# Row scales of the first output weights: sums of sizes on ScalarE in place of maxima on VectorE

## The chip, the cores and the metric

The kernel runs on one core of one Trainium2 chip. The metric is device time in microseconds (us) of one execution, median of three runs. Engines: TensorE (PE; its weight loads are PEld), VectorE (DVE), ScalarE (ACT), GpSimd (POOL), and SyncE (SP), whose queue issues the DMAs. Each engine works through its own queue of instructions.

## The reference

Attention over 4 batches and 12 heads, then two MLPs on the 1792 tokens. All inputs arrive as float64.

```python
q_n, k_n = rmsnorm(q, g_q), rmsnorm(k, g_k)              # 4 x 12 x 448 x 64
attn = softmax(q_n @ k_n.T / sqrt(64)); attn_out = attn @ v
x = attn_out.transpose(0, 2, 1, 3).reshape(1792, 768)
h = x @ w_in;  x = (h * sigmoid(1.702 * h)) @ w_out      # first MLP, 768 -> 2048 -> 768
h = x @ w_in2; x = (max(h, 0) + alpha * min(h, 0)) @ w_out2
```

## The kernel before

**Weights.** A float64 matrix is read as pairs of 32-bit words (DMA into a ring of raw tiles). `from_words` makes float32 of them: `fold`, a Prelu on ScalarE (L147), then a shift (L163) and a shift-and-or (L164) on VectorE. Each row of a weight matrix then gets a power of two as its scale: a maximum of the row's absolute values (L244, VectorE), `row_scales` (L104, L105 and L171, tiny VectorE operations), and `split_rows` writes the scaled row as two float16 halves, the high one on ScalarE (L178), the low one on VectorE (L179). When all rows are there, `weight_scales` takes the largest scale over partitions (a small TensorE matmul `pm`, L119) and makes a `ratio` for every row. The matmuls run three float16 products per pair (high-high, high-low, low-high).

**The first output weights** `w1o` are 2048 x 768: 16 row blocks of 128 x 768 (`nj` = 16), two loads each, in groups of two (`G1O`). Their generator `w1o_steps` is advanced while the second half of batch 0's attention runs, six pairs of heads with two units each. The float32 numbers of block j lie in the place of block j + 2 of `w1o`, so block j's own place is free by then.

**What else runs in that stretch.** For every unit: scores (PE `sp`, L490), their maxima (DVE `nm`, L504), the exponent (ACT `pr`, L523, with a sum read out), transposes (PE `tp`, L580), their copies (ACT `ptf`, L585), the values (PE `xp`, L616). Beside them `first_in` starts the first MLP on batch 0's first 256 tokens: it needs `x`, which `first_x` splits with the scale `first_sc` (DVE L646; ACT L139, DVE L140), then 18 matmuls `hp` (L720), a tanh (ACT `t`, L731) and a product (DVE `g`, L732) for each of 16 column blocks. After that the same for the other 192 tokens.

**The restart.** Batch 1's attention begins when q and k of its first pair have been squared and summed (ACT L395, DVE L397), their inverse roots computed on POOL (L398 to L408), scaled (DVE `qk`, L418), split (`hl`, ACT L451, DVE L452) and transposed by a DMA (`t<-hl`). Its first scores are `sp`, L499. At the same time VectorE and ScalarE split batch 0's `g` with the ratios of `w1o` (L809, L139, L140), for the second matmul `yp` (L790).

**Order.** The code is written as interleaved generators; the framework's scheduler then sets each engine's order when the program is built, from priorities and its own estimates of durations. A changed operation can therefore move others around it.

Of the kernel before, what the change touches and what calls it, by code (L numbers as in the profile page):

```python
# [13 lines left out]
AF = mybir.ActivationFunctionType  # L14
ALU = mybir.AluOpType
AX = mybir.AxisListType.X
# [28 lines left out]
R1O = 4  # L45
G1I = 1
G1O = 2
# [9 lines left out]
def attention_moe_kernel(  # L57
# [17 lines left out]
    nc = tc.nc  # L75
# [100 lines left out]
    def split_rows(w, num, inv, j):  # L176

        nc.scalar.activation(out=w[:, j, 0], in_=num, func=AF.Copy, scale=inv[:, j:j + 1])  # L178
        nc.vector.scalar_tensor_tensor(  # L179
            out=w[:, j, 1], in0=num, scalar=inv[:, j:j + 1], in1=w[:, j, 0], op0=ALU.mult, op1=ALU.subtract  # L180
        )
# [17 lines left out]
        done[nm] = mx, ratio  # L199
        yield  # L200

    def weights(src, nm, w, num_tile, raw_tile, parts, ahead, c, done, group, hold=0):


        rows, cols = src.shape
        words = src.bitcast(I32).rearrange("r (n t) -> r n t", t=2)
        nj = rows // 128
        m = cols // parts
        rm = const.tile([128, nj], F32, name=f"rm_{nm}")
        inv = const.tile([128, nj], F32, name=f"inv_{nm}")  # L210
        raws = []
        nums = []

        def load():
            t = len(raws)
            if t < nj * parts:
                j, i = divmod(t, parts)
                raw = raw_tile(t)
                src_words = words[j * 128:(j + 1) * 128, i * m:(i + 1) * m]
                if len(raw.shape) == 4:  # L220
                    src_words = src_words.rearrange("r (a n) t -> r a n t", a=raw.shape[1])
                loads.setdefault(nm, []).append(nc.sync.dma_start(out=raw, in_=src_words))
                raws.append(raw)

        def split_all():
            while nums:
                split_rows(w(), nums[0][1], inv, nums[0][0])
                nums.pop(0)
                yield

        for _ in range(ahead):
            load()
        yield
        for j in range(nj):
            if hold and j == hold:
                yield "held"
                yield from split_all()
            num = num_tile(j)
            for i in range(parts):
                from_words(num[:, i * m:(i + 1) * m], raws[j * parts + i])  # L240
                load()
                yield
            nums.append((j, num))
            nc.vector.tensor_reduce(out=rm[:, j:j + 1], in_=num, op=ALU.max, axis=AX, apply_absolute_value=True)  # L244
            if (j + 1) % group == 0:
                row_scales(rm, inv, slice(j + 1 - group, j + 1))
                yield
                if j >= hold:
                    yield from split_all()
        if hold:  # L250
            yield "rows"
        yield from weight_scales(nm, rm, nj, c, done, W2I_WAIT if hold else 0)

    def later_rows(w, d, other):

        nj = w.shape[1]
        return lambda j: w[:, j + d].rearrange("p e n -> p (e n)").bitcast(F32) if j + d < nj else other(j)

    scales = {}
# [884 lines left out]
    if True:  # L1144
# [10 lines left out]
        parts = stage[:, 0:R1I * 1024].bitcast(I32).rearrange("p (i n t) -> p i n t", i=R1I, t=2)  # L1155
# [7 lines left out]
        def num1o(j):  # L1163
# [7 lines left out]
        )  # L1171
        w1o_steps = weights(
            moe_w_out, "w1o", lambda: w1o, later_rows(w1o, 2, num1o), lambda t: raw1o[:, 4 * (t % R1O):4 * (t % R1O) + 4], 2,
            R1O, 2.0 ** -25, scales, G1O
        )
        next(w1i_steps)
        normalize(0)
# [43 lines left out]
        done = 4 * NP  # L1221
# [46 lines left out]
```

## Time and profile before

| | |
|---|---|
| time, median of 3 runs | 1184.49 us (1184.01 to 1185.91) |
| the profiled execution: its own time, its span | 1184.74 us, 1183.0 us |
| PE busy | 1073.3 us, 91% |
| DVE busy | 819.6 us, 69% |
| ACT busy | 673.3 us, 57% |
| POOL busy | 79.7 us, 7% |

The shares are averages over stages that are limited by different things. The `w1o` rows are made between about 105 and 206 us of the span, and that stretch has to be read by itself: in the view of stretches, where each engine's busy time stands for given bounds; in the timelines, where an idle time and what ended it stand in brackets; and in the groups by line, for the duration of one instruction.

### The profile page before, as it was taken

The page shows a single profiled execution, that of the slowest core. Times are in us where ns is not written, and L with a number is a line of the kernel's source. Part 1 is how long each engine was busy: PE and PEld are TensorE (multiplying, and loading weights), DVE is VectorE, ACT ScalarE, POOL GpSimd, SP SyncE. Part 2 cuts the span into 40 slices and gives each one's busy share as a digit, 9 for nine tenths or more (in the row PEclk, how much of TensorE's full clock was granted, in tenths as well). Part 3 has the DMA queues.
Part 4 walks back from the last instruction along what each step waited for, and adds up shares of the span by engine and source line. Part 5 has one row for each costly group of instructions (what it writes and reads, how often), then busy time and mean ns, then how long its engine had stood idle before and what let it go on. Part 6 is the DMA issues. An engine that isn't in the chain of part 4 may idle for free.

```text
span 1183.0 us, 18327 instructions
## 1 busy us (share of the span) xinstructions
PE 1073.3 (91%) x6755; PEld 586.6 (50%) x6755; DVE 819.6 (69%) x1445; ACT 673.3 (57%) x1348; POOL 79.7 (7%) x200
## 2 busy tenths in 40 slices
PE   3468799688789989999998999999999999999998
PEld 1234467554344444545454545544444467666665
DVE  6989999986767886467741868489996322978351
ACT  4667776787767875578742545256555423655220
POOL 2300001442011101100000000000000000000000
PEclk9579799899999999999998999999999999999999
DMA  7944542569888685666553821275624423353111
GB/s 232 266 144 137 150 135 77 113 138 182 160 158 157 136 157 121 122 122 115 93 128 65 307 92 52 99 255 178 224 78 144 142 72 123 99 173 101 34 30 31
DMA packets 256458, 158.06 MB, mean 134 GB/s; under 512 B 177648, under 2 KB 239728, under 8 KB 256368
## 3 DMA queue, kind: packets, MB, share of 16 engines
q1 hardware_dynamic: 256368, 156.89, 50.9%
q8 instruction: 53, 0.87, 0.3%
q14 instruction: 37, 0.30, 0.1%
HBM read 92.22 MB, written 25.69 MB: 100 GB/s over the span
## 4 chain that ended last, share of the span: by engine, by line
PE 32%; DVE 20%; DMA 10%; ACT 10%; issue 5%; SPq 3%; POOL 2%; ACTq 0%; POOLq 0%; DVEq 0%
PE op L1052 16%; PE h L892 7%; PE yp L790 5%; ACT pr L523 3%; DVE ph L592 3%; PE hp L767 3%; DVE nm L504 2%; ACT ph L565 2%; SPq L598 2%; DMA yr<-y_dram 2%; DMA qk<-in_q_dram 1%; DMA pt<-ph 1%; DMA t<-hl 1%; DVE g L140 1%; DMA vst<-in_v_dram 1%
## 5 line engine op out<-in xcount | busy, mean ns | idle before, releaser
L790 PE MATMUL yp<-g,w1o 128*128 128x448 f16 x1152 | 228.2, 355 | 1.9 <-DVE g L140 1.6
L892 PE MATMUL h<-x,w2i 128*128 128x512 f16 (+1 forms) x1152 | 218.9, 352 | 2.7 <-DVE pos L898 1.7
L767 PE MATMUL hp<-x,w1i 128*128 128x448 f16 x864 | 172.1, 356 | 3.7 <-DVE t L776 1.8
L892 PEld LDWEIGHTS <-w2i 128*128 128x128 f16 x1152 | 112.6, 98 | 108.1 <-issue 3.5
L790 PEld LDWEIGHTS <-w1o 128*128 128x128 f16 x1152 | 109.8, 98 | 111.8 <-issue 13.2
L767 PEld LDWEIGHTS <-w1i 128*128 128x128 f16 x864 | 82.8, 99 | 88.2 <-issue 15.7
L592 DVE SCALAR_TENSOR_TENSOR ph<-pr,sm,ph 128x448 f16<-128x448 f32 x126 | 86.9, 717 | 20.2 <-ACT ph L565 19.3
L504 DVE TENSOR_REDUCE nm<-sp 128x2 f32<-128x896 f32 x96 | 92.4, 963 | 0.4 <-PE sp L499 0.4
L523 ACT ACTIVATE pr<-sp,nm,c_s 128x448 f32<-128x448 f32 x126 | 90.0, 717 | 2.8 <-DVE ph L592 1.0
L897 ACT ACTIVATE pos<-h,sign 128x512 f32<-128x512 f32 (+1 forms) x64 | 40.2, 629 | 86.0 <-PE h L892 80.2
L565 ACT ACTIVATE ph<-pr,sm 128x448 f16<-128x448 f32 x126 | 77.8, 659 | 18.3 <-DVE sm L562 15.3
L1052 PEld LDWEIGHTS <-even 128*128 128x128 f16 x672 | 65.7, 98 | 43.4
L898 DVE SCALAR_TENSOR_TENSOR pos<-h,slope,pos 128x512 f32<-128x512 f32 (+1 forms) x64 | 43.4, 680 | 57.9 <-ACT pos L897 57.9
L720 PE MATMUL hp<-x,w1i 128*128 128x256 f16 (+1 forms) x576 | 63.9, 273 | 10.0 <-DVE t L732 4.8
L499 PE MATMUL sp<-t 64*128 64x448 f16 (+1 forms) x432 | 56.2, 365 | 17.0 <-ACT pr L523 17.0
L1052 PEld LDWEIGHTS <-odd 128*128 128x128 f16 x504 | 49.3, 98 | 32.6
L616 PE MATMUL xp<-pt,vs 128*64 128x256 f16 (+1 forms) x792 | 50.2, 271 | 16.6 <-DMA pt<-ph 8.4
L1052 PE MATMUL op<-w2lo,even 128*128 128x384 f16 x384 | 63.4, 326 | 0.0
L720 PEld LDWEIGHTS <-w1i 128*128 128x128 f16 x576 | 54.6, 103 | 17.5 <-issue 12.9
L140 DVE SCALAR_TENSOR_TENSOR g<-t,ratio_w1o,g 128x448 f16<-128x448 f32 x64 | 47.0, 736 | 15.0 <-ACT g L139 14.9
L506 ACT ACTIVATE nm<-nm,c_s 128x2 f32<-128x2 f32 x72 | 20.9, 290 | 62.4 <-DVE nm L504 62.2
L616 PEld LDWEIGHTS <-vs 128*64 128x64 f16 x792 | 39.3, 114 | 33.7 <-issue 18.7
(228 smaller groups left out, 1553.8 us busy)
## 6 DMA issues: line engine op xcount, KB each, us to landing
g<-in_moe_w_in_dram SPq DMA_DIRECT2D x24, 512.0 KB, 5.7
g<-in_moe_w_out_dram SPq DMA_DIRECT2D x32, 384.0 KB, 3.7
w2raw<-in_moe_w_in_dram SPq DMA_DIRECT2D x24, 512.0 KB, 5.6
w2raw<-in_moe_w_out_dram SPq DMA_DIRECT2D x16, 768.0 KB, 6.3
g_dram<-pos SPq DMA_DIRECT2D x48, 256.0 KB, 2.0
gp<-g_dram SPq DMA_DIRECT2D x8, 1024.0 KB, 6.7
odd<-g_dram SPq DMA_DIRECT2D x6, 1024.0 KB, 5.4
y_dram<-y SPq DMA_DIRECT2D x24, 224.0 KB, 2.5
```

What stands on the lines that cost most here:

```text
L140: nc.vector.scalar_tensor_tensor(out=dst[1], in0=src, scalar=scale, in1=dst[0], op0=ALU.mult, op1=ALU.subtract)
L499: nc.tensor.matmul(out=sp[:, j, 0:S] if n == 2 else sp[ds, 0, 0:S], lhsT=qt[ds] if n == 2 else qt[ds, 64:128], rhs=kt[ds, 0:S], start=(i = ...
L504: nc.vector.tensor_reduce(out=nm[:, 0:n], in_=sp[:, 0:n, 0:S], op=ALU.max, axis=AX, negate=True)
L523: nc.scalar.activation(out=pr[i], in_=sp[:, i, 0:S], func=AF.Exp, bias=nm[:, i:i + 1], scale=c_s if u >= 4 * NP else 1.0, accum_out=sm[:, ...
L565: nc.scalar.activation(out=ph[:, i, 0:S], in_=pr[i], func=AF.Copy, scale=sm[:, i:i + 1])
L592: nc.vector.scalar_tensor_tensor(out=ph[:, i, S:2 * S], in0=pr[i], scalar=sm[:, i:i + 1], in1=ph[:, i, 0:S], op0=ALU.mult, op1=ALU.subtract)
L616: nc.tensor.matmul(out=xp[64 * j:64 * j + 64, t:t + n], lhsT=vs[ks, j, c], rhs=pt[ks, kc, o:o + n], start=(i == 0), stop=(i == len(steps) ...
L720: nc.tensor.matmul(out=ps, lhsT=w1i[:, kk, e, m * 128:(m + 1) * 128], rhs=xs[0, kk][:, f, cols], start=(i == 0), stop=(i == 3 * KD - 1))
L767: nc.tensor.matmul(out=ps, lhsT=w1i[:, kk, e, m * 128:(m + 1) * 128], rhs=x[:, f], start=(n == 0), stop=(n == 3 * KD - 1))
L790: nc.tensor.matmul(out=ps, lhsT=w1o[:, m, e, j * 128:(j + 1) * 128], rhs=g[:, m, f], start=(n == 0), stop=(n == 3 * KF - 1))
L892: nc.tensor.matmul(out=ps, lhsT=w2i[:, kk, e, m * 128:(m + 1) * 128], rhs=x2[kk][:, f], start=(c == 0), stop=(c == 3 * KD - 1))
L1052: nc.tensor.matmul(out=ps, lhsT=ops[:, o, m, f], rhs=rhs[:, e], start=(c == 0), stop=(c == 3 * KH - 1))
```

## The change

For `w1o` alone (`sizes=True`), the row's measure is no longer its largest absolute value. ScalarE runs one Abs with a factor 0.5 over the 128 x 768 float32 row block and adds its results along the row into `rm`, through its accumulator. The float16 output of that instruction is put in block j's own place in `w1o` and is overwritten later by the split. `row_scales` and all that follows stay as they are; the scales come out as another power of two. The other weights keep the maximum.

```diff
-    def weights(src, nm, w, num_tile, raw_tile, parts, ahead, c, done, group, hold=0):
+    def weights(src, nm, w, num_tile, raw_tile, parts, ahead, c, done, group, hold=0, sizes=False):
...
             nums.append((j, num))
-            nc.vector.tensor_reduce(out=rm[:, j:j + 1], in_=num, op=ALU.max, axis=AX, apply_absolute_value=True)
+            if sizes:
+                nc.scalar.activation(out=w()[:, j, 0], in_=num, func=AF.Abs, scale=0.5, accum_out=rm[:, j:j + 1])
+            else:
+                nc.vector.tensor_reduce(out=rm[:, j:j + 1], in_=num, op=ALU.max, axis=AX, apply_absolute_value=True)
...
         w1o_steps = weights(
             moe_w_out, "w1o", lambda: w1o, later_rows(w1o, 2, num1o), lambda t: raw1o[:, 4 * (t % R1O):4 * (t % R1O) + 4], 2,
-            R1O, 2.0 ** -25, scales, G1O
+            R1O, 2.0 ** -25, scales, G1O, sizes=True
         )
```

The scheduler sets the rest anew. From the first removed maximum (about 112 us of the span before) to about 455 us the order of most engines' instructions differs; before and after that it is the same. Lines behind the edit stand 3 higher in the changed kernel (L646 is L649, L720 is L723); the sum is L245.

**Place 1, VectorE ahead of `first_sc`**, the scale of batch 0's `x`. Before:

```order
L735 TENSOR_SCALAR c_y<-mv,mx_w1i 128x1
L630 TENSOR_TENSOR xraw<-xp,xraw 128x256
L244 TENSOR_REDUCE rm_w1o<-w1o 128x1 x2
L164 SCALAR_TENSOR_TENSOR w1o<-g_143,w1o 128x384
L112 RECIPROCAL av<-av 128x1
L738 TENSOR_SCALAR c_t<-c_y 128x1
L531 TENSOR_SCALAR sums<-sums 128x3
L104 TENSOR_SCALAR rm_w1o<-rm_w1o 128x2
L163 TENSOR_SCALAR w1o<-w1o 128x384
L504 TENSOR_REDUCE nm<-sp 128x2
L163 TENSOR_SCALAR w1o<-w1o 128x384
L504 TENSOR_REDUCE nm<-sp 128x1
```

The next row there is L646, `first_sc`. With the change:

```order
L738 TENSOR_SCALAR c_y<-mv,mx_w1i 128x1
L164 SCALAR_TENSOR_TENSOR w1o<-g_143,w1o 128x384 x2
L633 TENSOR_TENSOR xraw<-xp,xraw 128x256
L163 TENSOR_SCALAR w1o<-w1o 128x384
L112 RECIPROCAL av<-av 128x1
L741 TENSOR_SCALAR c_t<-c_y 128x1
L164 SCALAR_TENSOR_TENSOR w1o<-g_143,w1o 128x384
L649 TENSOR_SCALAR first_sc<-ratio_w1i,av 128x6
```

The two maxima are gone from it, and the two `nm` now stand behind `first_sc`; a pair of L164 that stood ahead of `c_y` stands behind it.

**Place 2, ScalarE ahead of the first `x`.** Before:

```order
L523 ACTIVATE pr,sums<-sp,nm 128x448
L147 ACTIVATE w1o<-g_143 128x384 x3
L139 ACTIVATE x<-xraw,first_sc 128x256 x3
L585 ACTIVATE ptf<-tp 128x2x2x64
L178 ACTIVATE w1o<-w1o,inv_w1o 128x768 x2
```

With the change:

```order
L526 ACTIVATE pr,sums<-sp,nm 128x448
L245 ACTIVATE w1o,rm_w1o<-w1o 128x768
L147 ACTIVATE w1o<-g_143 128x384
L139 ACTIVATE x<-xraw,first_sc 128x256 x3
L147 ACTIVATE w1o<-g_143 128x384 x2
L588 ACTIVATE ptf<-tp 128x2x2x64 x2
```

A sum has come in, and two of the three folds (L147) stand behind the first `x`. Of the 16 sums two stand ahead of the first `x`, twelve between it and the tenth tanh of the 256-token pass, two behind that.

**Place 3, TensorE at the restart** (`hp` of 192 tokens; `t_1931` is the transposed tile of batch 1's first pair). Before, around the small matmul of `weight_scales`:

```order
L720 MATMUL hp<-x,w1i 128x192
L119 LDWEIGHTS ones
L119 MATMUL pm<-diag,ones 128x128
L720 LDWEIGHTS w1i
L720 MATMUL hp<-x,w1i 128x192
```

With the change, at the same place:

```order
L723 MATMUL hp<-x,w1i 128x192
L502 LDWEIGHTS t_1931
L502 MATMUL sp<-t_1931 128x448
L502 LDWEIGHTS t_1931
L502 MATMUL sp<-t_1931 128x448
```

Before, 54 more `hp` followed `pm` and only then the first 12 score matmuls of batch 1 (18 in one piece). With the change ten of these stand ahead of `pm` and two behind it, and the 54 `hp` follow.

## Rows read from the trace of the kernel before

**Rows 1.** Busy time by stretch: us, PE, PEld, DVE, ACT, POOL, PEclk, DMA share, GB/s.

```profile
105.00:126.10 21.10, 14.48 (x96) 6.70 (x95) 18.84 (x52) 15.65 (x37) 0.00 (x0) 0.89 0.52 150
126.10:184.00 57.90, 55.34 (x404) 35.90 (x404) 53.58 (x128) 44.35 (x101) 0.00 (x0) 0.92 0.50 144
184.00:206.30 22.30, 20.45 (x210) 17.74 (x209) 20.10 (x41) 13.51 (x27) 4.17 (x14) 1.00 0.16 40
206.30:249.20 42.90, 30.59 (x300) 23.70 (x299) 38.81 (x75) 34.47 (x83) 18.09 (x23) 0.88 0.62 130
...
250.00:455.00 205.00, 181.66 (x1268) 90.14 (x1267) 157.57 (x280) 152.47 (x361) 35.20 (x86) 0.98 0.78 154
455.00:1183.00 728.00, 711.61 (x4207) 382.38 (x4205) 444.16 (x707) 349.62 (x619) 3.66 (x14) 0.99 0.42 120
```

**Rows 2.** Timeline of PE, 105 to 210 us: start, duration, instruction, idle before.

```profile
126.11 0.37 PE L720 MATMUL hp<-x,w1i 128*128 128x256 f16 x1 [3.49 <-ACT x L139]
```

**Rows 3.** Timeline of DVE, 105 to 210 us.

```profile
120.78 1.80 DVE L244 TENSOR_REDUCE rm_w1o<-w1o 128x1 f32<-128x768 f32 x2
122.50 0.55 DVE L164 SCALAR_TENSOR_TENSOR w1o<-g,w1o 128x384 int32<-128x384 int32 x1
...
123.49 1.08 DVE L504 TENSOR_REDUCE nm<-sp 128x2 f32<-128x896 f32 x1
...
125.29 0.22 DVE L646 TENSOR_SCALAR first_sc<-ratio_w1i,av 128x6 f32<-128x6 f32 x1
```

**Rows 4.** Timeline of ACT, 105 to 210 us.

```profile
121.06 0.57 ACT L147 ACTIVATE w1o<-g 128x384 f32<-128x384 f32 x1
123.39 0.55 ACT L147 ACTIVATE w1o<-g 128x384 f32<-128x384 f32 x1 [1.76 <-DMA g<-in_moe_w_out_dram]
124.50 0.56 ACT L147 ACTIVATE w1o<-g 128x384 f32<-128x384 f32 x1 [0.57 <-DMA g<-in_moe_w_out_dram]
125.55 1.31 ACT L139 ACTIVATE x<-xraw,first_sc 128x256 f16<-128x256 f32 x3 [0.49 <-DVE first_sc L646]
126.95 0.38 ACT L585 ACTIVATE ptf<-tp 128x256 f32<-128x256 f32 x1
127.23 1.75 ACT L178 ACTIVATE w1o<-w1o,inv_w1o 128x768 f16<-128x768 f32 x2
128.88 0.37 ACT L585 ACTIVATE ptf<-tp 128x256 f32<-128x256 f32 x1
```

**Rows 5.** Groups by line and form, whole span: count | busy us, mean ns of one.

```profile
L523 ACT ACTIVATION_READ_ACCUMULATOR pr<-sp,nm 128x1 f32 x42 | 9.3, 222 | 0.0
...
L244 DVE TENSOR_REDUCE rm_w1o<-w1o 128x1 f32<-128x768 f32 x14 | 13.1, 943 | 0.0
...
L178 ACT ACTIVATE w1o<-w1o,inv_w1o 128x768 f16<-128x768 f32 x14 | 12.3, 928 | 0.5 <-DVE inv_w1o L171 0.5
```

**Rows 6.** Timeline of ACT at one exponent: the read-out starts, the next copy starts.

```profile
129.66 0.21 ACT L523 ACTIVATION_READ_ACCUMULATOR pr<-sp,nm 128x1 f32 x1
129.75 0.91 ACT L139 ACTIVATE x<-xraw,first_sc 128x256 f16<-128x256 f32 x2
```

**Rows 7.** Busy time by stretch, two later stretches of 10 us, as rows 1.

```profile
250.00:260.00 10.00, 10.00 (x70) 5.19 (x69) 9.91 (x16) 9.09 (x23) 9.02 (x15) 1.00 0.74 146
...
390.00:400.00 10.00, 8.77 (x68) 4.55 (x67) 9.73 (x18) 9.72 (x25) 2.89 (x7) 1.00 0.50 101
```

**Rows 8.** Timeline of PE at the restart, 196 to 262 us.

```profile
204.81 1.65 PE L720 MATMUL hp<-x,w1i 128*128 128x192 f16 x18 [1.39 <-DVE g L732]
...
206.35 4.62 PE L720 MATMUL hp<-x,w1i 128*128 128x192 f16 x54
210.90 1.31 PE L499 MATMUL sp<-t 64*128 64x448 f16 x12
217.93 1.30 PE L499 MATMUL sp<-t 64*128 64x448 f16 x6 [5.72 <-ACT pr L523]
219.91 3.04 PE L720 MATMUL hp<-x,w1i 128*128 128x192 f16 x18 [0.68 <-DVE t L732]
```

**Rows 9.** The chain that ended last, 100 to 215 us: start, us, what.

```profile
200.54 2.09 DVE qk L418 x2
202.63 1.86 DVE w1o L179 x2
...
206.39 4.27 DMA t<-hl
```

## The prediction

> **What bounds the kernel now.** I read the stretches first, because the shares of the whole span hide the place that matters. From 105 to 206 us, where the `w1o` rows are made, VectorE is busy 18.8 of 21.1, 53.6 of 57.9 and 20.1 of 22.3 us [rows 1]: about nine tenths throughout, and all 16 maxima lie there. ScalarE is busy 15.7, 44.4 and 13.5 us, 73.5 of 101.3 together. TensorE is near full only in the second and third piece (55.3 of 57.9, 20.5 of 22.3); in the first it has 14.5 of 21.1. Then the timelines, to see which wait ends last. TensorE's longest wait there, 3.49 us, ends at 126.11 with the first `x` from ScalarE [rows 2]; ScalarE had waited for weight loads (1.76 and 0.57 us) and then for VectorE's `first_sc` [rows 4]; and ahead of `first_sc` on VectorE stand two maxima [rows 3]. The next place is the restart: after 12 score matmuls TensorE stands still for 5.72 us until the exponents of the first unit are done [rows 8]. From 250 us on TensorE has 181.7 of 205, then 711.6 of 728 us. A gain made before 250 us should mostly live to the end, since nothing later starts at a fixed time.
>
> **The change, part by part.** All sums go against the profiled execution's own 1184.74 us; the median of the runs stands 0.25 us below it.
>
> *Prices.* A maximum takes 943 ns [rows 5]; two of them hold VectorE from 120.78 to 122.50, so 0.86 us each [rows 3], and 16 take 13.8 us off VectorE. A sum isn't in the trace. Its nearest row is the split's high half, the same 128 x 768 float32 read and float16 written: 928 ns [rows 5], and the row of two such (127.23) is followed at 128.88 by the next instruction, so 0.83 us of the queue each [rows 4]. The accumulator's read-out takes 222 ns as a row [rows 5] but only 0.09 us of the queue (129.66 to 129.75) [rows 6]. I take 0.92 us for a sum, 14.7 us for 16; the ends are 0.83 (read-out wholly hidden) and 0.83 + 0.22 = 1.05. So the change moves nearly its own weight from one engine to the other. The Trainium skill's page "ScalarE: Activation LUTs", section "What ACT_TABLE_LOAD costs", makes an instruction with immediate scale 93 ns cheaper than one whose scale is a pointer, as the split's is; by that the sum would cost 0.83 us with its read-out and the twelve sums of step 2 about 1.1 us less, a time of 1177.4 where I say 1178.5. No row here has an Abs, so I keep the row's price.
>
> *Step 1, the first `x`: 3.0 us earlier.* With the change both maxima and both `nm` are out of the way of `first_sc`. What goes is 122.50 - 120.78 = 1.72 and 125.29 - 123.49 = 1.80 us [rows 3]; the pair of L164 that now stands behind `c_y` instead of ahead of it changes nothing. `first_sc` comes at 125.29 - 3.52 = 121.8. ScalarE is then the later one: free at 121.06, a sum to 121.98, one fold (0.47 to the next instruction) to 122.45 and the first `x` starts there instead of at 125.55 [rows 4]: 3.1 us, of which I count 3.0. The loads that ScalarE waited for now delay the other two folds, behind the `x`. Bounds: 0, if the one fold left ahead is the one that waits for its load, and 3.5, the whole wait of TensorE [rows 2].
>
> *Step 2, 126 to 184 us: 1 us lost.* Twelve sums fall between the first `x` and the tenth tanh, which is this stretch: ScalarE goes from 44.4 to 44.4 + 12 x 0.92 = 55.4 of 57.9 us, 96%; VectorE goes down by 11 maxima x 0.86 = 9.5 us to 44. So ScalarE takes VectorE's place as the engine next to TensorE. What that costs is not in the trace. Best case: TensorE's idle 57.9 - 55.3 = 2.6 us closes [rows 1]. Worst case: TensorE waits for whatever stands behind each sum, 12 x 0.92 - 2.6 = 8.4 us. Two later stretches are nearest: at 91% ScalarE, TensorE is busy all 10 us; at 97% it has 8.77 of 10 [rows 7]. The mean, 0.6 us idle in 10, is 3.6 us in 57.9; 2.6 are there already, so 1 us is lost.
>
> *Step 3, 184 to 206 us: 1 us gained.* Two sums fall there or behind, ScalarE has 13.5 of 22.3 us, so they are covered by its 8.8 idle us; without that cover they would cost 1.8. TensorE waits 1.39 us for a `g` [rows 8] that stands behind `qk` and the two late splits L179 on VectorE (200.54 to 204.49) [rows 9]. With the change `qk` runs ahead of the last 256-token product, and I count 1 of these 1.39 us. Bounds 0 and 1.85, all of TensorE's idle time there.
>
> *Step 4, the restart: 3 us gained.* Before, 54 `hp` run from 206.35 to 210.9, then the scores, then the 5.72 us wait [rows 8]. With the change the scores stand ahead of the 54 `hp`, which then fill the wait: at most 210.90 - 206.35 = 4.55 us. That needs the transposed tile early. It lands at 206.39 + 4.27 = 210.66 now [rows 9], and `qk` and `hl` move two `hp` groups forward and past the splits that held `hl` back, so I expect it in time. But VectorE has 38.8 of 42.9 us from 206 to 249 [rows 1], 4.1 idle, so it can't give all 4.55 unless work moves ahead of the stretch. I take 3; bounds 0 (the tile is late and the 54 `hp` stand behind it) and 6, if TensorE, busy again, also keeps its clock: the granted clock of that stretch is 0.88 [rows 1], and 18 `hp` took 3.04 us at 219.9 against 1.65 at 204.8 [rows 8].
>
> *Step 5, the rest: 0.* From 250 to 455 us the order is shuffled without a purpose I can find; TensorE is idle 23.3 of 205 us there [rows 1]. I count 0, with 2.5 either way. Behind 455 us the order is the same.
>
> SP's and POOL's queues issue what they issued; no DMA is added, and the ring of raw tiles is freed by L164, a little earlier.
>
> Sum: -3.0 + 1.0 - 1.0 - 3.0 = **-6.0 us**, 1178.7 for the profiled execution and **1178.5** for the median.
>
> **The rivals.**
>
> *ScalarE becomes the bound (slower).* In step 2 each sum stands in ScalarE's queue ahead of a copy, an exponent or a tanh that TensorE waits for. At its worst that loses 8.4 us; the `hl` copy stands in the same queue, so the tile is late and step 4 gives 0. Then -3.0 + 8.4 - 1.0 = +4.4: 1188.9. It decides once a sum holds TensorE for more than (2.6 + 3.0 + 1.0) / 12 = 0.55 us. For it: 96% of a queue is much; TensorE already waits for ScalarE's copies. Against it: the order puts many sums behind the copies, and at 91% ScalarE cost TensorE nothing [rows 7]. The Trainium skill's page "ScalarE: Activation LUTs", section "Rules for kernel authors", speaks for this rival: it keeps simple arithmetic on VectorE, which it calls faster per element. The trace doesn't bear that out for this tile, 943 against 928 ns [rows 5].
>
> *Hidden anyway (no change).* TensorE is nearly full from 126 to 206 us and VectorE from 206 to 249. Step 1 is given back in step 2 (3.6 us lost instead of 1), step 3 gives 1 and step 4 nothing: about -0.4, 1184.1.
>
> *VectorE was the bound throughout (much faster).* Then the whole 13.8 us count: 1170.7. For it: nine tenths busy from 105 to 249 us. Against it: TensorE has only 1.85 + 2.6 us idle from 126 to 206.
>
> **How the numbers follow.** The forecast 0.50, VectorE's full gain 0.10, hidden 0.18, ScalarE the bound 0.22. A measurement of this kernel can tell about 0.2%, 2.4 us, from no change. The first two are faster: 0.60; same 0.18; slower 0.22. The forecast's own range, with steps 1 to 5 not all at one end, is 1174 to 1182. The range for 8 in 10 reaches to the slower rival's centre nearly and cuts off most of the full VectorE gain: 1172 to 1188, with a tenth left out at either end.
>
> **What would show it.** Right: the first `hp` starts near 123 us; from there to the tenth tanh ScalarE is over 90% busy and the stretch is no longer than 59 us; the first L502 scores begin ahead of the last 54 `hp` and the wait for the exponent behind them is under 2 us; a sum's row is near 0.93 us with a read-out of 0.2; all of the difference stands at 250 us and stays. Wrong: TensorE's waits for `ptf`, `pr` or tanh grow by several us between 126 and 184; TensorE stands before the first L502 waiting for `t<-hl`; or the gain is there at 250 us and gone at 455.

## The result, and the profile after

The changed kernel is slower: 1199.2 us median of 6 runs (1195.9 to 1201.3) against 1185.86 us (1184.0 to 1187.0) of the kernel before, ratio 1.0115, 95% interval 1.0099 to 1.0132. I had said 1178.5. The profiled execution took 1201.32 us, span 1199.5. One execution of sums_old_order, further down, took 3793 us and is left out of its ratio. In the rows below the tanh is L734, the product L735, the scores of batch 1 L502 and their maxima L507.

Busy time by stretch of the changed kernel, cut as [rows 1] (us, PE, PEld, DVE, ACT, POOL, PEclk, DMA share, GB/s):

```profile
105.00:126.10 21.10, 18.14 (x111) 8.40 (x111) 18.54 (x50) 19.93 (x49) 0.00 (x0) 0.92 0.55 163
126.10:184.00 57.90, 49.31 (x366) 31.88 (x366) 43.69 (x113) 49.66 (x117) 0.00 (x0) 0.91 0.48 136
184.00:206.30 22.30, 19.16 (x166) 15.04 (x165) 14.84 (x28) 14.43 (x30) 4.33 (x14) 0.92 0.20 53
206.30:249.20 42.90, 25.41 (x263) 19.74 (x260) 36.55 (x69) 30.63 (x71) 16.23 (x21) 0.80 0.57 111
250.00:455.00 205.00, 180.49 (x1282) 92.67 (x1280) 153.74 (x274) 148.64 (x352) 32.40 (x75) 0.95 0.77 150
455.00:1183.00 728.00, 713.50 (x4232) 382.60 (x4231) 452.53 (x727) 361.18 (x645) 8.51 (x28) 1.00 0.43 122
```

The load went where it was meant to go: from 126 to 184 us VectorE has 43.7 us instead of 53.6, ScalarE 49.7 instead of 44.4. But TensorE lost too, 49.3 instead of 55.3, and from 206 to 249 us 25.4 instead of 30.6. The sum's own groups, by line and form:

```profile
L245 ACT ACTIVATE w1o<-w1o 128x768 f16<-128x768 f32 x14 | 11.9, 850 | 1.9 <-DVE w1o L164 1.3 <-DVE w1o L179 0.7
...
L245 ACT ACTIVATION_READ_ACCUMULATOR w1o<-w1o 128x1 f32 x14 | 2.9, 205 | 0.0
```

One of the sums in the timeline of ACT, up to the next instruction:

```profile
121.80 0.85 ACT L245 ACTIVATE w1o<-w1o 128x768 f16<-128x768 f32 x1
122.53 0.21 ACT L245 ACTIVATION_READ_ACCUMULATOR w1o<-w1o 128x1 f32 x1
122.63 0.55 ACT L147 ACTIVATE w1o<-g 128x384 f32<-128x384 f32 x1
```

What TensorE waited for from 126 to 206 us (us in total, times, longest), where before its longest wait behind the first hp was 1.4 us:

```profile
PE rp L549 <- ACT ptf L588: 4.9, 2, 2.7
PE hp L723 <- DVE g L735: 3.7, 2, 3.1
PE rp L549 <- DVE g L735: 1.6, 1, 1.6
```

And the timeline of PE at the restart, to be laid beside [rows 8]:

```profile
212.74 1.12 PE L502 MATMUL sp<-t 64*128 64x448 f16 x10 [0.29 <-DMA t<-hl]
213.79 0.23 PE L119 MATMUL pm<-diag,ones 128*128 128x128 bf16 x1
...
215.11 3.13 PE L723 MATMUL hp<-x,w1i 128*128 128x192 f16 x36 [0.79 <-DVE g L735]
...
220.13 0.74 PE L502 MATMUL sp<-t 64*128 64x448 f16 x6
...
227.97 1.30 PE L502 MATMUL sp<-t 64*128 64x448 f16 x6 [5.28 <-ACT pr L526]
237.31 3.04 PE L723 MATMUL hp<-x,w1i 128*128 128x192 f16 x18 [8.05 <-DVE t L735]
```

The scores do stand ahead of the 54 hp now, and the third unit's scores follow the 54 hp at 220.13 us without a wait for an exponent. But two more units now stand ahead of the ninth 192-token product: the fifth unit's scores wait 5.28 us, and the ninth product waits 8.05 us for VectorE's work on the sixth. To place the loss I followed the same matmul through both timelines of PE. An hp product is 18 matmuls, so of the hp matmuls of batch 0 the 217th begins the thirteenth 256-token product, and the 361st, 433rd and 451st begin the fifth, ninth and tenth 192-token product. The first comes 2.1 us earlier than before, the 217th 7.5 us later, the 361st 6.0 later, the third unit's scores 2.2 later (217.93 before [rows 8]), the 433rd 17.4 later, the 451st 15.5 later; the first yp is 21.9 us later, and from the next batch's hp on 13 to 17 us stay. So there were two suspects: the load between 126 and 190 us, and the restart.

### The profile page after: what moved, and what is told of

Same layout as the page of the kernel before. It is cut to its first block, busy times and chain, and to the rows that moved or that the text cites. A ratio compares the mean times of both kernels' runs of the same rounds, so it can differ in the third digit from the quotient of the medians.

```text
span 1199.5 us, 18346 instructions
## 1 busy us (share of the span) xinstructions
PE 1077.6 (90%) x6755; PEld 588.0 (49%) x6755; DVE 808.5 (67%) x1429; ACT 686.2 (57%) x1380; POOL 79.4 (7%) x200
## 4 chain that ended last, share of the span: by engine, by line
PE 40%; DVE 21%; DMA 14%; ACT 12%; issue 6%; SPq 5%; POOL 2%; ACTq 0%; POOLq 0%; DVEq 0%
PE op L1055 16%; PE h L895 9%; PE yp L793 6%; ACT pr L526 4%; DVE nm L507 3%; DVE ph L595 3%; PE hp L770 3%; DMA qk<-in_q_dram 2%; DMA vst<-in_v_dram 2%; PE xp L619 2%; SPq L601 2%; DVE g L140 2%; DMA g<-in_moe_w_out_dram 2%; DMA g<-in_moe_w_in_dram 2%; ACT ph L568 1%
## 5 line engine op out<-in xcount | busy, mean ns | idle before, releaser
L595 DVE SCALAR_TENSOR_TENSOR ph<-pr,sm,ph 128x448 f16<-128x448 f32 x126 | 83.8, 691 | 20.7 <-ACT ph L568 20.0
L507 DVE TENSOR_REDUCE nm<-sp 128x2 f32<-128x896 f32 x96 | 92.3, 963 | 4.8 <-PE sp L502 4.4
L901 DVE SCALAR_TENSOR_TENSOR pos<-h,slope,pos 128x512 f32<-128x512 f32 (+1 forms) x64 | 43.4, 680 | 60.1 <-ACT pos L900 60.1
L723 PE MATMUL hp<-x,w1i 128*128 128x256 f16 (+1 forms) x576 | 66.3, 277 | 14.6 <-DVE t L735 9.7
L502 PE MATMUL sp<-t 64*128 64x448 f16 (+1 forms) x432 | 56.6, 364 | 16.5 <-ACT pr L526 16.2
L723 PEld LDWEIGHTS <-w1i 128*128 128x128 f16 x576 | 55.2, 104 | 27.5 <-issue 22.1
L619 PE MATMUL xp<-pt,vs 128*64 128x256 f16 (+1 forms) x792 | 50.8, 275 | 18.5 <-DVE x L140 10.8
L1055 PEld LDWEIGHTS <-odd 128*128 128x128 f16 x504 | 49.3, 98 | 32.6
```

What stands on the lines that cost most here:

```text
L502: nc.tensor.matmul(out=sp[:, j, 0:S] if n == 2 else sp[ds, 0, 0:S], lhsT=qt[ds] if n == 2 else qt[ds, 64:128], rhs=kt[ds, 0:S], start=(i = ...
L507: nc.vector.tensor_reduce(out=nm[:, 0:n], in_=sp[:, 0:n, 0:S], op=ALU.max, axis=AX, negate=True)
L595: nc.vector.scalar_tensor_tensor(out=ph[:, i, S:2 * S], in0=pr[i], scalar=sm[:, i:i + 1], in1=ph[:, i, 0:S], op0=ALU.mult, op1=ALU.subtract)
L619: nc.tensor.matmul(out=xp[64 * j:64 * j + 64, t:t + n], lhsT=vs[ks, j, c], rhs=pt[ks, kc, o:o + n], start=(i == 0), stop=(i == len(steps) ...
L723: nc.tensor.matmul(out=ps, lhsT=w1i[:, kk, e, m * 128:(m + 1) * 128], rhs=xs[0, kk][:, f, cols], start=(i == 0), stop=(i == 3 * KD - 1))
L1055: nc.tensor.matmul(out=ps, lhsT=ops[:, o, m, f], rhs=rhs[:, e], start=(c == 0), stop=(c == 3 * KH - 1))
```

## The experiments

All ratios are to the kernel before on the same chip, where it took 1184.6 to 1186.1 us; the table is the summary. "Order" says whose order of instructions holds up to some 205 us, and behind it; "units" is how many attention units of batch 1 (six score matmuls each) TensorE's order has ahead of the ninth 192-token product; the next two columns are when the 217th hp matmul comes, and the time from the 361st to the first yp, read from the profiled timeline of PE.

| kernel | measure | order to 205 / behind | units | 217th hp | 361st hp to yp | time us | ratio, 95% |
|---|---|---|---|---|---|---|---|
| before | maxima | before / before | 3 | 188.4 | 44.4 | 1185.9 | 1 |
| changed | sums | changed / changed | 5 | 195.9 | 60.3 | 1199.2 | 1.0115 (1.0099 to 1.0132) |
| none_before_order | none | before / before | 3 | 185.2 | 44.4 | 1184.3 | 0.9991 (0.9977 to 1.0005) |
| sums_before_loose | sums | before, `w1o` rows on VectorE free / before | 3 | 190.0 | 44.5 | 1186.5 | 1.0004 (0.9989 to 1.0019) |
| sums_load_after | sums | changed / before | 3 | 194.0 | 43.7 | 1186.5 | 1.0005 (0.9991 to 1.0018) |
| none_load_after | none | changed / before | 3 | 193.9 | 44.0 | 1186.8 | 1.0008 (0.9993 to 1.0023) |
| none_load_before | none | before / changed | 5 | 186.2 | 63.2 | 1198.2 | 1.0105 (1.0076 to 1.0135) |
| none_after_order | none | changed / changed | 5 | 194.3 | 58.8 | 1195.6 | 1.0090 (1.0065 to 1.0115) |
| maxima_after_order | maxima | changed / changed | 5 | 192.7 | 59.9 | 1198.8 | 1.0114 (1.0091 to 1.0137) |
| sum64_after_order | short sums | changed / changed | 5 | 196.8 | 59.2 | 1202.9 | 1.0145 (1.0111 to 1.0178) |
| sums_scales_first | sums | changed / one piece moved | 5 | 195.0 | 61.5 | 1201.9 | 1.0116 (1.0084 to 1.0148) |
| none_after_pe_load_before | none | PE of before / changed | 5 | 195.4 | 60.1 | 1197.7 | 1.0099 (1.0060 to 1.0138) |
| sums_old_order | sums | changed / own | 3 | 195.3 | 50.8 | 1193.3 | 1.0070 (1.0051 to 1.0090) |
| sums6_old_order | 6 sums | own / own | 4 | 188.3 | 53.9 | 1188.5 | 1.0038 (1.0021 to 1.0054) |
| no_measure_old_order | none | own / own | 4 | 188.8 | 53.5 | 1193.3 | 1.0070 (1.0050 to 1.0089) |
| maxima_new_order | maxima | before / own | 6 | 186.2 | 61.7 | 1196.3 | 1.0088 (1.0063 to 1.0112) |
| maxima_scores_later | maxima | before / own | 0 | 189.2 | 40.4 | 1195.9 | 1.0084 (1.0056 to 1.0112) |
| maxima_scores_latest | maxima | before / own | 0 | 188.1 | 34.0 | 1207.2 | 1.0183 (1.0160 to 1.0206) |
| sums_scores_later | sums | changed / own | 0 | 196.8 | 42.3 | 1211.5 | 1.0218 (1.0191 to 1.0244) |
| sums_scores_latest | sums | changed / own | 0 | 192.0 | 34.4 | 1207.1 | 1.0186 (1.0152 to 1.0221) |

One thing to keep in mind for the columns from single profiles: maxima_new_order is the kernel before, instruction for instruction, up to some 204 us, and its 217th hp came 2.2 us earlier; maxima_scores_later is too, and its 217th hp came 0.8 us later. So 3 us lie between executions.

### Load or restart: the first scores moved

The scheduler that orders this program works from its own estimate of when each instruction is ready, so an edit at one place moves others. A dependency of order alone, without a wait, holds one piece in place. In sums_old_order the first scores of batch 1 go behind the eighth 192-token product on TensorE, as before:

```diff
-                scores(us[i])
+                u = us[i]
+                with tc.issue_after(last_hp[7, S - FIRST].ins) if u == 4 * NP else ExitStack():
+                    scores(us[i])
...
```

> The change as it is, but the first scores of batch 1 are queued on TensorE behind the eighth 192-token product, as they stood before; up to that point all engines' orders are those of the changed kernel. Theory LOAD (the sums lengthen 126 to 190 us by filling ScalarE and adding a hop to each row, and that is carried to the end): the 217th hp matmul about 7.5 us later than in the kernel before, as in the changed kernel, and 1192 to 1196 us. Theory ORDER (the loss is what the scheduler made of the restart at 205 to 245 us): the delay of 7.5 us is taken up in the 5.72 us wait at the restart, and 1184 to 1188 us. If both hold, about 1193 us, with no wait of 8 us for the product L735's counterpart near 237 us.

Measured 1193.3, ratio 1.0070, its 217th hp 6.9 us late: LOAD's range and LOAD's sign, and the time named for both together. It looked like a loss of the load stage; sums_load_after, further down, will show that it isn't. maxima_new_order does the reverse to the kernel before: two units' scores are traced earlier, and the partition maximum's matmul and the later hp matmuls are held behind them.

> VectorE's maxima as in the kernel before, but the first twelve score matmuls of batch 1 stand ahead of the partition maximum's matmul and of the sixth 192-token product, about as in the changed kernel (there ten ahead of the one, twelve ahead of the other). Up to there all orders are those of the kernel before. LOAD: 1184 to 1188 us, no different from before, since no load is moved. ORDER: the 8.05 us wait for a 192-token product appears here too, and 1193 to 1199 us.

Measured 1196.3, within ORDER's range. Order alone, with the old maxima, costs some 10 us (ratio 1.0088). The next kernel takes the measure out, with the first scores held behind the eighth product (`nc.gpsimd.memset(rm[:, j:j + 1], 0.125)` in the place of the sum):

> Leaves out the measure of the rows: neither maxima nor sums, each row's number is a constant set by GpSimd (so the two small VectorE operations on each pair of rows no longer wait for anything). Restart in the order of the kernel before. LOAD: with neither load the 217th hp matmul comes at least 5 us earlier than before and the time is 1174 to 1180 us; the distance to sums_old_order, some 15 us, is the price of the sums, that to the kernel before the price of the maxima. ORDER: the restart's wait takes up most of the gain, 1181 to 1186 us, and sums_old_order lies within 4 us of it.

Measured 1193.3, above both ranges. This is the run that changed my mind: with the measure left out and only GpSimd's 16 constants added, the kernel is 8 us slower than before. Its order was the suspect then. The restart wasn't quite that of before: in this kernel and the next, four units stand ahead of the ninth product, not three. And the mix:

> Sums on ScalarE for the first six rows only, maxima on VectorE for the other ten; restart in the order of the kernel before. LOAD: the early gain (first hp 2 us earlier, the 73rd 5 us) is had and the loss comes only where sums go on, so the 217th hp matmul is 0 to 5 us earlier than before and the time is 1180 to 1186 us, 7 us or more below sums_old_order. ORDER: no more than 2 us from sums_old_order.

Measured 1188.5, in neither theory's range, its 217th hp where it was before. LOAD's early gain is there at the 73rd hp (5.2 us) and gone at the 217th.

### The order held as a list

To take load and order apart, the next kernels carry the whole order as a list, each engine's instructions by their place in the program text, and hold it:

```diff
+    def keep_order():
+        traced = {}
+        for ins in tc.nc.cur_bb.bb.instructions:
+            if ins.name not in measures and "Boundary" not in type(ins).__name__:
+                traced.setdefault(str(ins.engine), []).append(ins)
+        behind = mybir.DependencyInfo(mybir.DependencyClass.NoSync, mybir.DependencyReason.DATA)
+        for engine, runs in ORDER.items():
+            mine = [traced[engine][k] for a, n in runs for k in range(a, a + n)]
...
+            for one, two in zip(mine, mine[1:]):
+                tc.add_manual_dep(two, one.name, behind, reason="order")
```

Only the measure floats, and is a maximum, a sum, a sum of 64 columns (`num[:, 0:64]`) or a constant.

> Leaves out the measure: each row's number is a constant that GpSimd sets, and the 16 maxima are gone. Every other instruction of every engine stands in exactly the order of the kernel before (its order is written into the kernel as a list and held). It prices 13.8 us of VectorE work by itself. Theory ORDER (the time between 126 and 250 us is set by the order the scheduler made, not by the measure's load): within 3 us of the kernel before, 1182 to 1188 us, because TensorE was 97% busy from 150 to 190 us. Theory LOAD: at least 6 us faster, 1172 to 1179 us, and no_measure_old_order's 1193 was an accident of its own order.

> Leaves out the measure in the same way; every other instruction stands in exactly the order of the changed kernel. ORDER: it keeps most of the loss without any sum in it, 1193 to 1200 us. LOAD: the sums' 13 us of ScalarE are gone, so the 217th hp matmul falls back from 7.5 us late to no later than before, and the time to 1184 to 1190 us.

> Maxima on VectorE as before, and every other instruction in exactly the order of the changed kernel. ORDER: as slow as the changed kernel or slower, 1196 to 1206 us. LOAD: the load stage is that of the kernel before, only the restart's order is lost, 1188 to 1194 us.

> Sums over the first 64 of a row's 768 numbers (leaves out the other 704), all else and the whole order as in the changed kernel: the step by way of ScalarE stays, its time shrinks from 0.84 us to an estimated 0.2 us a row. If the time that ScalarE spends in the sums holds TensorE: 1186 to 1192 us, like none_after_order. If the waits between the two engines do (VectorE's scales wait for ScalarE's sum, ScalarE's split waits for the scales): still above 1195 us while none_after_order is lower. ORDER: both stay above 1193 us.

All four times lie in ORDER's ranges. The 13.8 us of maxima taken off VectorE at an unchanged order give 0.9991, no gain that can be told. The changed kernel's order costs 10.0 us without any measure, 13.2 with the old maxima and 13.3 with the sums; short sums are no better than whole ones. That sum64_after_order (four executions, 1198.9 to 1206.4) lies above none_after_order (1194.8 to 1199.2) is also what its text names for waits between the two engines. So in the changed order some 3 us may hang on having a measure at all; most of the loss doesn't. Busy time by stretch of none_before_order shows why the maxima cost nothing:

```profile
126.10:184.00 57.90, 55.32 (x421) 36.01 (x420) 45.10 (x117) 44.69 (x104) 0.00 (x0) 0.95 0.54 149
184.00:206.30 22.30, 20.91 (x222) 19.07 (x221) 18.86 (x44) 12.42 (x24) 4.17 (x14) 1.00 0.21 49
```

VectorE falls from 53.58 to 45.10 us, and TensorE stays at 55.3 of 57.9 [rows 1]. TensorE was the engine that was full.

The missing cell is sums in the order of before:

> The sums on ScalarE as in the changed kernel, but the order of the kernel before: TensorE, ScalarE (but for the sums), GpSimd and the transfers stand in exactly that order, VectorE too but for its 88 operations on the rows of the first output weights, which the scheduler places round the sums (the sum's written place is that of two rows earlier, so it can't come before that row's split, and the old order of those operations can't be kept with it). ORDER: the sums by themselves cost nothing that can be told, 1182 to 1188 us. LOAD: 1191 to 1197 us, and the 217th hp matmul 5 us or more later than before.

Measured 1186.5, ratio 1.0004. TensorE, ScalarE and GpSimd run in the order of before here; VectorE does but for its operations on these rows. So the change as such, maxima out of VectorE and sums into ScalarE, is worth nothing that can be told at the order of before. What the sums_before_loose text says of the written place is a second thing that the diff hides: the sum writes where the numbers of an earlier row block lie, so it waits for that block's split (L179 in the sum's group above, 0.7 us in all).

### Which part of the order

The sets of instructions ahead of some 205 us are the same in both kernels, so the two lists can be cut there and joined crosswise.

> Leaves out the measure (constants). Order of the kernel before up to some 205 us, then that of the changed kernel; the sets of instructions on either side of the cut are the same in both. Prices the restart's order alone: 1190 to 1197 us, with the 8 us wait for the sixth 192-token product, if the restart's order costs by itself; 1183 to 1187 us if all of none_after_order's 10 us come from the load stage.

> Leaves out the measure. The reverse: order of the changed kernel up to some 205 us, then that of the kernel before. Prices the load stage's order alone: 1189 to 1194 us, 217th hp matmul about 5.6 us late as in none_after_order, if the lateness is carried to the end; 1183 to 1187 us if the restart's waits take it up.

> The changed kernel with its sums and its order up to some 205 us, then exactly the order of the kernel before. If the sums' lateness before the restart (217th hp matmul 7.5 us late) is taken up by the restart's waits, as the 5.2 us of none_load_after were: 1185 to 1189 us. If it is carried to the end: 1191 to 1195 us, as sums_old_order.

The restart's order alone costs 12 us: 1198.2, a little above the range that was named for it. Timeline of PE, first of none_load_before, then of none_before_order, which has the same load stage and the old restart:

```profile
208.61 2.05 PE L756 MATMUL sp<-t 64*128 64x448 f16 x10 [4.33 <-DMA t<-hl]
...
216.81 0.74 PE L756 MATMUL sp<-t 64*128 64x448 f16 x6
...
225.23 1.30 PE L756 MATMUL sp<-t 64*128 64x448 f16 x6 [5.87 <-ACT pr L780]
234.32 3.04 PE L977 MATMUL hp<-x,w1i 128*128 128x192 f16 x18 [7.79 <-DVE t L989]
```

```profile
214.53 1.30 PE L755 MATMUL sp<-t 64*128 64x448 f16 x6 [5.33 <-ACT pr L779]
216.50 3.04 PE L976 MATMUL hp<-x,w1i 128*128 128x192 f16 x18 [0.66 <-DVE t L988]
```

With the changed restart TensorE stands 4.33 us for the transposed tile, which the changed kernel, late by then, hardly waits for (0.29). The third unit's scores come 2.3 us later (216.81 and 214.53) and the ninth product 17.8 us later (234.32 and 216.50). So most of the price arises between these two points, where TensorE's order has two more units.

The load stage's order alone, with constants or with sums, ends 0.7 and 0.5 us above before, inside what can be told, though the 217th hp comes 5 us late. Timeline of PE of sums_load_after, where that lateness goes:

```profile
210.38 4.62 PE L974 MATMUL hp<-x,w1i 128*128 128x192 f16 x54
214.93 1.31 PE L753 MATMUL sp<-t 64*128 64x448 f16 x12
220.50 1.30 PE L753 MATMUL sp<-t 64*128 64x448 f16 x6 [4.25 <-ACT pr L777]
...
252.53 6.97 PE L1044 MATMUL yp<-g,w1o 128*128 128x448 f16 x36
```

It shrinks, if not evenly: 5.6 us at the 217th hp, 4.0 at the 54 hp (206.35 before [rows 8]), 2.6 at the third unit's scores, whose wait for an exponent is 4.25 us instead of 5.72, 3.3 at the first yp (249.19 before), up to 4.6 in the next batch's hp, and 1.3 to 3.1 in the hp of the batches behind it, no more than executions differ by.

One of the places where the load stage loses its 5 us can be seen in two kernels with the same work and no measure. Timeline of PE, first none_before_order, then none_after_order:

```profile
163.52 0.44 PE L836 MATMUL tp<-identf,pr 128*128 128x128 f32 x2
163.89 0.44 PE L802 MATMUL rp<-identf,sums 128*64 128x128 f32 x4
164.26 0.33 PE L798 MATMUL rp<-identf,sums 64*64 64x64 f32 x4
164.54 2.13 PE L976 MATMUL hp<-x,w1i 128*128 128x256 f16 x18
```

```profile
163.29 0.44 PE L834 MATMUL tp<-identf,pr 128*128 128x128 f32 x2
165.58 0.44 PE L800 MATMUL rp<-identf,sums 128*64 128x128 f32 x4 [1.85 <-ACT ptf L839]
165.95 0.33 PE L796 MATMUL rp<-identf,sums 64*64 64x64 f32 x4
166.21 1.24 PE L870 MATMUL xp<-ptf,w1o 128*64 128x192 f32 x8
```

In the first, 18 hp follow and cover ScalarE's copies of the transposes; in the second the hp came before, and TensorE waits 1.85 us for them. I tried TensorE's order of before alone:

> Leaves out the measure. Order of the changed kernel on every engine, but up to some 205 us TensorE alone stands in the order of the kernel before (where 18 hp matmuls stand between a unit's transposes and its values, in the changed kernel ahead of the transposes). If what costs in the load stage is that TensorE's order no longer covers ScalarE's copies of the transposes: the 217th hp matmul no more than 1 us late and the time 3 to 6 us below none_after_order, 1189 to 1193 us. If it is ScalarE's own order (folds of later rows, which wait for their transfers, ahead of the copies): 217th hp matmul 4 us late or more and 1194 to 1200 us.

Measured 1197.7, its 217th hp at 195.4, 7.0 us late: later, not earlier. TensorE's order by itself doesn't mend the load stage. Both numbers are those named for ScalarE's own order, but no run changed ScalarE's list alone, so which list loses the 5 us is not shown.

### What in the restart's order

The trace of the changed kernel suggested a chain to me: the ratios of the output weights came at 220.82 us instead of 208.01, the splits that need them hold both t buffers, and so the sixth product is late. Its timeline of DVE, then one row of POOL:

```profile
216.69 1.08 DVE L507 TENSOR_REDUCE nm<-sp 128x2 f32<-128x896 f32 x1
...
218.21 0.28 DVE L120 TENSOR_REDUCE mx_w1o<-pm 128x1 f32<-128x128 f32 x1
218.41 1.08 DVE L507 TENSOR_REDUCE nm<-sp 128x2 f32<-128x896 f32 x1
...
220.82 0.69 DVE L198 TENSOR_SCALAR ratio_w1o<-rm_w1o,wrmx 128x16 f32<-128x16 f32 x1
...
228.77 3.85 DVE L140 SCALAR_TENSOR_TENSOR g<-t,ratio_w1o,g 128x448 f16<-128x448 f32 x2
...
236.93 0.33 DVE L735 SCALAR_TENSOR_TENSOR t<-t,hp 128x192 f32<-128x192 f32 x1
...
238.38 1.26 DVE L140 SCALAR_TENSOR_TENSOR g<-t,ratio_w1o,g 128x448 f16<-128x448 f32 x2
```

```profile
228.43 3.71 POOL L421 TENSOR_TENSOR qk<-qk,rs 128x896 f32<-128x896 f32 x2
```

sums_scales_first edits the list of the changed kernel: in that stretch of TensorE, VectorE and ScalarE the scales' chain, the first splits and the sixth tanh and product come first, attention behind them.

> The changed kernel with its sums and its order, but for one stretch at the restart: the chain of the output weights' common scale (partition maximum's matmul, maximum, reciprocal, ratios), the splits of the first products that need the ratios, and the sixth 192-token tanh and product stand ahead of attention's maxima, exponents and divisions that were queued before them. Theory: the late ratios hold both t buffers, and so the sixth product, which TensorE waited 8.05 us for; then that wait falls below 4 us and the time to 1186 to 1193 us. If it is the amount of attention in that stretch, wherever it stands: still 1195 us or more, with a wait for scores or values in the place of that for the product.

My theory fell: 1201.9. The timeline of its PE has the wait in another place:

```profile
214.17 4.62 PE L973 MATMUL hp<-x,w1i 128*128 128x192 f16 x54 [1.06 <-DVE g L985]
224.87 1.30 PE L752 MATMUL sp<-t 64*128 64x448 f16 x6 [6.08 <-ACT pr L776]
227.07 1.33 PE L752 MATMUL sp<-t 64*64 64x448 f16 x6 [0.90 <-ACT pr L776]
231.42 1.30 PE L752 MATMUL sp<-t 64*128 64x448 f16 x6 [3.02 <-ACT pr L776]
232.66 2.41 PE L973 MATMUL hp<-x,w1i 128*128 128x192 f16 x18
...
238.64 1.30 PE L752 MATMUL sp<-t 64*128 64x448 f16 x6 [2.12 <-ACT pr L776]
```

The 8.05 us for the product are gone, and four waits for exponents, 12.1 us together, stand in their place. Five units are scored before the ninth product; in these two kernels, whichever comes first on VectorE and ScalarE, TensorE waits for the other. The table goes with it, as a correlation: with three units ahead the stretch from the 361st hp to the first yp takes 44 us in five kernels (51 in sums_old_order), with four 54, with five 59 to 63, with six 62.

Does it go on downwards? Four kernels hold the first scores behind the ninth or tenth product (`last_hp[8, ...]`, `last_hp[9, ...]` in the edit of sums_old_order):

> The kernel before with its maxima; the first scores of batch 1 are queued on TensorE behind the ninth 192-token product (before: behind the eighth), and the scheduler orders the rest: two units ahead of the tenth product, a third after three more. Theory UNITS (each attention unit scored ahead of the 192-token products delays them by 8 to 10 us, of which most reaches the end): the stretch from the 361st hp matmul to the first yp falls from 44 to 36 us or less, and the time to 1174 to 1182 us. Rival DUE LATER (attention that is moved back comes due behind 250 us, where TensorE then waits for it): 1184 to 1192 us.

> As maxima_scores_later, but queued behind the tenth product: three score matmuls ahead of the eleventh, nine more behind the thirteenth. UNITS: the stretch to the first yp is 32 us or less, 1170 to 1180 us. DUE LATER: the first yp comes 10 us or more earlier, but by the first hp of the next batch nothing is left of it, 1186 us or more.

> The changed kernel with its sums, the first scores queued behind the ninth product as in maxima_scores_later. UNITS: within 4 us of maxima_scores_later, 1174 to 1184 us, since the sums by themselves cost nothing once the restart's order is good. DUE LATER: 1184 to 1194 us.

> The changed kernel with its sums, the first scores queued behind the tenth product (five score matmuls ahead of the thirteenth, since the scheduler places them later still). UNITS: 1170 to 1182 us. DUE LATER: 1186 us or more.

UNITS fell as a rule for the time: all four are slower, by 10 to 25 us. DUE LATER had the direction, though two of its ranges were too low (1195.9 and 1211.5). The stretch does shrink, to 40 to 42 and 34 us, and the first yp of maxima_scores_latest comes 10.6 us earlier; but the 289th yp comes 16.8 us later. Busy time of that later stretch, first of the kernel before, then of maxima_scores_latest:

```profile
300.00:350.00 50.00, 40.50 (x299) 19.87 (x298) 32.83 (x65) 34.14 (x85) 4.30 (x14) 0.97 0.81 156
```

```profile
300.00:350.00 50.00, 31.63 (x206) 15.52 (x205) 36.44 (x72) 34.64 (x86) 4.71 (x14) 0.73 0.85 170
```

Attention that is put off comes due there: TensorE stands idle for 18 of 50 us, all of it waiting for attention's own tiles (9.4 us for exponents, 3.6 for a `t<-hl`), at a granted clock of 0.73. No order run here is faster than that of the kernel before.

## Why the prediction was wrong, point by point

**Prices: right, at the low end of the bounds.** The sum's rows have a median of 844 ns, and from the sum at 121.80 to the next instruction at 122.63 are 0.83 us with the read-out of 0.2. The Trainium skill's "ScalarE: Activation LUTs", section "What ACT_TABLE_LOAD costs", was the better guide: its immediate scale, 93 ns below the split's 928, gives an estimate of 835, and the trace agrees with 844. For the time it didn't matter.

**What bounds: wrong, and this is why a lighter VectorE was forecast to gain.** I read VectorE's nine tenths from 105 to 206 us as the bound, with TensorE "near full". TensorE was the bound from 126 to 206, and none_before_order puts the price on the maxima: without them, at the same order, the time is 1.4 us lower by the medians, and the ratio's interval includes 1. My rival "Hidden anyway", 0.18, is what the change by itself does: 1.0004 in sums_before_loose. I had its arithmetic and ranked it third.

**Step 1, first x 3.0 us earlier:** 2.1 by the trace, within the bounds; but maxima_new_order, with all maxima in place, had its first hp at 124.5, where the changed kernel's is at 124.0 and before's at 126.1, so most of it may be the one execution I measured from. What an early start is worth is not shown: none_before_order's first hp comes 1.9 us earlier and its profile stays some 3 us ahead to the end, but over all its executions the gain is the 1.4 us above, which can't be told from none.

**Step 2, 1 us lost:** 9.6 lost, from -2.1 at the first hp to +7.5 at the 217th, over my worst case of 8.4. The cause was wrong too. I had ScalarE 96% busy; from the first hp to the tenth tanh are 63.0 us, and it is busy for 85% of them. With constants in place of the sums the changed order loses 8.3 (from -2.4 to +5.9), so the stage's order cost what I had put down to the sums. Yet this isn't the step that made the kernel slower: behind it the old restart takes up all that can be told (sums_load_after, 1.0005), and with the changed restart it adds nothing (none_after_order 1.0090, none_load_before 1.0105). My tenth tanh was misplaced as well: before, it starts at 179.8 us and not at 184.

**Step 3, 1 us gained:** 1.5 by the trace, from +7.5 at the 217th hp to +6.0 at the 361st; the 1.39 us wait is gone. As for step 2, it doesn't reach the end.

**Step 4, 3 us gained: the step that failed.** It took the restart's new order for a gain of 3 us and priced it by one filled wait. The runs show a loss of 12 us from that order alone, without any sum or maximum in the kernel (none_load_before, 1.0105). Two things in the step were wrong. The first is the tile that I expected in time: in none_load_before TensorE stands 4.33 us for it, my own sign of being wrong, and the third unit's scores come 2.3 us later than with the old restart. Behind the changed load stage the tile hardly holds TensorE (0.29 us in the changed kernel), and without a measure the third unit's scores come 1.8 us earlier with the changed restart than with the old one (none_after_order, none_load_after): the filled wait is worth that at most. The second is larger. I left out the rest of the same reordering: ahead of the ninth product the new order has 30 score matmuls where the old one has 18, and on VectorE five maxima of scores instead of two ahead of the sixth product. I noted that VectorE had only 4.1 idle us there, and never priced the work moved in front. In none_load_before the ninth product comes 17.8 us later than with the old restart. That the two more units are the reason is argued, not shown: sums_scales_first, with the sixth product ahead of the maxima, was no faster.

**Step 5, the rest 0:** of the 21.9 us at the first yp some 6 are given back by 455 us, outside my 2.5.

**"ScalarE becomes the bound"** had the right sign (+4.4, chance 0.22), and signs named for it came true: waits for ptf grew, the stretch lengthened. It is wrong as the cause all the same: sum64_after_order has sums of 0.25 us instead of 0.84 and gains nothing, and sums_before_loose keeps the sums and loses nothing that can be told. A rival can be borne out by its signs and still not be what happened. The rule that the prediction sets beside it, from the Trainium skill's "ScalarE: Activation LUTs", section "Rules for kernel authors", gives its figure for bf16; the 943 and 928 ns are of float32 rows and don't speak against it.

**Still open:** which instructions of the restart's order matter. TensorE's order is not all of it: sums_old_order and sums_load_after have the same load stage and, up to some 241 us, the same order on TensorE, and yet the first is some 8 us slower. They part on VectorE and ScalarE at 209 to 213 us. In sums_old_order the second `hl` stands on VectorE ahead of two products `g`, and it waits for ScalarE's half, which waits for the first transpose to land; TensorE waits for one of these `g`:

```profile
214.42 4.62 PE L727 MATMUL hp<-x,w1i 128*128 128x192 f16 x54 [2.59 <-DVE g L740]
...
225.29 1.30 PE L502 MATMUL sp<-t 64*128 64x448 f16 x6 [5.01 <-ACT pr L526]
```

The third unit's scores come 4.8 us later than in sums_load_after (220.50), so a good part of the 8 us is there before TensorE's orders part. The changed restart has this too: in none_load_before ScalarE stands 7.66 us for the DMA `t<-hl` ahead of the second `hl`, with two tanhs queued behind it; in none_before_order, where the tanhs and two splits of `g` come first, 1.51 us. No run moves the second `hl` alone, so its share isn't measured, and VectorE's list of one kernel with TensorE's of the other wasn't run either.

## What to carry to other kernels

Where a scheduler orders the program, compare orders first: the change's own cost here is 0.0004 of the time, less than can be told, that of the order it set off 0.0090 without any measure in the kernel, and 0.0105 for the restart's part of it; these two can't be told apart. Hold the old order and make the change alone; if a kernel with the work simply left out is no faster at the old order, the work was hidden. And a piece moved ahead into a wait has to be priced with everything that moves with it, on the engine that is short of time there.

## What the runs showed of the hardware that I had not expected

While GpSimd multiplied qk at 228.43 to 232.1 us, two splits on VectorE took 3.85 us; ten us later, with GpSimd idle, two of the same form took 1.26. The Trainium skill's "Trainium Architecture — The Big Picture", section "What this means for kernel authors", says that VectorE and GpSimd contend for a shared port pair, by an exclusive lock; the trace agrees that they hold each other up, here by a factor of three; that it is a lock, no row here shows. The kernel before has such a meeting too: at 227.87 us two products L592 on VectorE took 2.94 us while GpSimd multiplied qk, where a single one took 0.67 us at 225.76. So whether it is any part of the 12 us isn't shown.

A wait can also make the work behind it dearer. Right behind the 8.05 us wait, 18 hp of 192 tokens took 3.04 us at a granted clock of 0.50; in [rows 8] the same 18 took 1.65 us at 204.81, where the clock was 1.00: the two levels, 1.2 and 2.4 GHz. The mean of 206 to 249 us fell from 0.88 to 0.80. The ninth product, though, ran at 0.50 in the kernel before too, at 219.91 us, soon behind the wait of 5.72, so these 1.4 us are not part of the difference.
